# Neighbourhood attention on one core: key tiles of 9 row slots by 14 columns instead of 16 by 8

## The chip, the core and the metric

The kernel runs on one core of a Trainium2 chip. A core has a matrix engine (TensorE, PE in the profile, with its weight loads shown as PEld), a vector engine (VectorE, DVE), a scalar engine (ScalarE, ACT), GpSimd (POOL) and SyncE (SP). Each works through its own list of instructions in the order in which the kernel issues them, and they wait for each other through semaphores. [...] Transfers to and from HBM are issued by SP, POOL or ACT and are carried out by 16 DMA engines. The metric is the device time of one execution in microseconds, median over several runs.

## The reference

```
qkv = x @ wqkv                          # x: 224 x 224 x 192, bfloat16
r0 = clip(i - 6, 0, 224 - 1 - 12)       # first key row of query row i; columns alike
key rows    r0 + 0, 2, ..., 12          # 7 rows, dilation 2
key columns c0 + 0, 2, ..., 12          # 7 columns
logits = q . k * 192 ** -0.5            # 49 keys per query
p = softmax(logits)
out = (sum of p * v) @ wo
```

The keys of a query all have one row parity and one column parity. Rows 0 to 5 share the window that begins at row 0, and the last rows the one that begins at row 211.

## The kernel before

**Classes.** `rc` is the parity of the key rows, `cc` that of the key columns. Each class has 112 key rows (and columns) and 112 query rows: in the interior those of its own parity, at one border a few of the other parity too. Two neighbouring columns are folded into one position of 384 channels (three times 128), so that there are `S` = 112 positions in a row.

**Scores.** The weights are folded first: A = Wq·Wkᵀ·scale (the tiles `aw`), so that a logit is (x_q·A)·x_k and the keys are x itself. Keys lie with channels on partitions in `XA` (128 channels) and `XB` (64 channels and 64 rows of one-hot marks). Query products x_q·A lie in `GA` and `GB`; in `GB` the partitions beside the one-hot marks hold 0 or -30000, so the same two matmuls that make a logit also mask keys outside the window. A key tile has 16 row slots by 8 columns, 128 keys. A step treats 8 query rows of one class. Their windows need 14 key rows; two blocks of 8 rows form a ring of 16 slots. A key tile meets the queries of 8 + 6 = 14 positions: 14 x 8 = 112 columns of a matmul. `s_group` (L399, L400) computes four tiles into one PSUM bank, and ACT takes the exponential (L403). 14 tiles for each column class make seven such groups per step.

**Values.** `XN` holds x with keys on partitions. `y_unit` (L418) multiplies tile after tile with the exponentials and adds the overlapping position windows up in PSUM, for half of the positions, one column class and one part `kt` of the channels. There are eight such units per step; each is copied into `ysb` by ACT or DVE (L424). `o_mm` (L436) multiplies that by Wv·Wo (`WP`), whose further column gives the sum of the exponentials; DVE takes the reciprocal (L440) and multiplies (L451) into `o_sb`, which SP stores.

**Query products.** `g_piece` makes them in three pieces per step (kinds 0, 1, 2: L343, L351), and ACT and DVE copy them from PSUM (L355 to L365): kinds 0 and 2 to `GA` by ACT, the two halves of kind 1 to `GB` by DVE. Outermost positions pair with positions of the other column class, and are computed apart in `edge_item` (L287) and spread by `edge_copies`, with ACT (L321, L324) and POOL (L322, L323).

**Loads.** x comes in twice: transposed by SP into `xt` (L91), from which DVE and ACT copy the keys of a new block into `XA` and `XB` (`key_copy`, L269, L271), and straight into `XN` by POOL and SP (L103), 14 DMAs per block of 8 rows.

**PSUM.** Three pools have two buffers each: `ps_s` for scores, `ps_y` for y, and `ps_go`, whose buffers have two banks each, for query products, edge products and the projection's pieces in turn. A buffer is written again only when its copy has ended.

**Order.** The schedule is by hand: the instructions go to each engine in the order in which the Python loop emits them, and waits follow from that. The loop runs over 28 steps, the two row classes in turn. In each of the seven groups of a step stand one `s_group`, then a query piece or (L563 to L565) a piece of the step before's projection, and then one or two y units of tiles whose exponentials are done (`run_y`), so that PE meets S, a job, y, S, a job, y.

Of the kernel before, what the change touches and what calls it, by code (L numbers as in the profile page):

```python
# [7 lines left out]
BF = mybir.dt.bfloat16  # L8
# [8 lines left out]
BR = 8  # L17
KC = 8
QW = KC + HALO
NEG = -30000.0  # L20
XP = 448
SLOTS = 16
NO = 7
H0 = 63
# [3 lines left out]
def kernel(  # L28
# [11 lines left out]
    NJ = H // 16  # L40
    NK = S // KC
    SR = H // 2
# [23 lines left out]
    gkeys = [(rc, p, 0) for rc in range(2) for p in range(2)] + [(0, 0, 1), (1, (NJ - 1) % 2, 1)]  # L66
    GA, GB = {}, {}
    for gk in gkeys:
        for cc in range(2):
            if gk[2] == 0:  # L70
                GA[gk[:2] + (cc,)] = const.tile([128, S, BR], BF, name="ga%d%d%d" % (gk[:2] + (cc,)))
            GB[gk + (cc,)] = const.tile([128, S, BR], BF, name="gb%d%d%d%d" % (gk + (cc,)))

# [4 lines left out]
    def gkey(rc, j):  # L78
        border = (rc == 0 and j == 0) or (rc == 1 and j == NJ - 1)
        return (rc, j % 2, int(border))  # L80
# [4 lines left out]
    def load_xt(b, part):  # L85
        if not 0 <= b < NJ:
            return
        if b not in xt:
            xt[b] = xt_pool.tile([128, 3, 16, S], BF, name=f"xt{b}", tag="xt")
        r = 4 * part  # L90
        nc.sync.dma_start_transpose(out=xt[b][:, :, r:r + 4, :].rearrange("p t r c -> p t (r c)"),  # L91
                                    in_=xp[16 * b + r:16 * b + r + 4].rearrange("r j c -> (r j) c"))

    DOWN = list(range(NK - 1, -1, -1))

    def load_xn(eng, rc, m, tiles):

        if not 0 <= m < NJ:
# [11 lines left out]
    for part in range(4):  # L110
        load_xt(0, part)
    for part in range(4):
        load_xt(1, part)
    load_xn(nc.sync, 0, 1, DOWN[:7])
    for part in range(4):
        load_xt(2, part)
    load_xn(nc.sync, 1, 1, DOWN[:5])
# [5 lines left out]
    gorder = [(0, 0, 1), (1, 0, 0), (0, 1, 0), (1, 1, 0), (0, 0, 0), (1, (NJ - 1) % 2, 1)]  # L123
    assert sorted(gorder) == sorted(gkeys)
    i_r = const.tile([128, len(gorder), BR], I32, name="i_r")

# [5 lines left out]

# [4 lines left out]
    for gi, (rc, p, brd) in enumerate(gorder):  # L137
        j = (0 if rc == 0 else NJ - 1) if brd else 2 + p
        ws = [max(BR * j + i - HALO, 0) if rc == 0 else min(BR * j + i, SR - WIN) for i in range(BR)]
        for (a, n_, first, step) in _affine(ws):  # L140
            io(i_r[:, gi, a:a + n_], n_, first % 16, step, 16)


# [14 lines left out]
    t_r = const.tile([128, SLOTS], BF, name="t_r")  # L158
    rowT = const.tile([128, SLOTS, KC], BF, name="rowT")
    cm = const.tile([128, S], BF, name="cm")  # L160
    cmE = const.tile([128, S, BR], BF, name="cmE")
    rm = const.tile([128, len(gorder), BR], BF, name="rm")
    nc.vector.tensor_single_scalar(out=i_c[:], in_=i_c[:], scalar=31, op=ALU.bitwise_and)
    nc.vector.tensor_single_scalar(out=t_c[:], in_=i_c[:], scalar=0.0, op=ALU.is_equal)
    nc.vector.tensor_single_scalar(out=t_r[:], in_=i_c[:, 0:SLOTS], scalar=0.0, op=ALU.is_equal)
    nc.vector.tensor_copy(out=rowT[:], in_=t_r[:].unsqueeze(2).to_broadcast([128, SLOTS, KC]))
    nc.vector.tensor_single_scalar(out=i_m[:], in_=i_m[:], scalar=31, op=ALU.bitwise_and)
    nc.vector.tensor_scalar(out=cm[:], in0=i_m[:], scalar1=float(HALO) + 0.5, scalar2=NEG, op0=ALU.is_gt, op1=ALU.mult)
    nc.vector.tensor_copy(out=cmE[:], in_=cm[:].unsqueeze(2).to_broadcast([128, S, BR]))
    nc.vector.tensor_single_scalar(out=i_r[:], in_=i_r[:], scalar=15, op=ALU.bitwise_and)  # L170
    nc.vector.tensor_scalar(out=rm[:], in0=i_r[:], scalar1=float(HALO) + 0.5, scalar2=NEG, op0=ALU.is_gt, op1=ALU.mult)

    def onehots(eng, cc, rc):
# [5 lines left out]
        eng.tensor_copy(out=XB[cc][rc][c_].rearrange("p n (r c) -> p n r c", c=KC),  # L179
                        in_=t_c[c_].rearrange("p (n c) -> p n c", c=KC).unsqueeze(2).to_broadcast([32, NK, SLOTS, KC]))  # L180
        eng.tensor_copy(out=XB[cc][rc][r_],
                        in_=rowT[r_].rearrange("p r c -> p (r c)").unsqueeze(1).to_broadcast([32, NK, 128]))

    def masks(eng, gi, ccs=(0, 1)):
        for cc in ccs:
            g = GB[gorder[gi] + (cc,)]
            eng.tensor_copy(out=g[CROW[cc]], in_=cmE[CROW[cc]])
            eng.tensor_copy(out=g[RROW[cc]], in_=rm[RROW[cc], gi, :].unsqueeze(1).to_broadcast([32, S, BR]))

    def grp_copy(eng, rc):  # L190
        eng(out=XN[rc][:, 0:NK * XP].rearrange("p (n c) -> p n c", c=XP)[:, :, 0:64],
            in_=grp[:].unsqueeze(1).to_broadcast([128, NK, 64]))
        eng(out=XN[rc][:, NK * XP:], in_=grp[:])

    onehots(nc.vector, 0, 0)
    masks(nc.vector, 0, (0,))
# [464 lines left out]
```

## Time and profile before

| | us |
|---|---|
| median of 3 runs (331.49 to 335.01) | 334.75 |
| profiled execution: its span, first to last instruction | 332.4 |
| PE busy | 314.8 |
| DVE busy | 269.1 |
| ACT busy | 249.9 |
| POOL busy | 212.5 |

No time of the profiled execution other than its span is given. Busy time of PE runs from the first start to the modelled end of each matmul, which overlap; how fast PE really works is read from the starts of consecutive matmuls. "A <- B: total, times, longest" in the list of waits is idle time of A's engine that ended when B did. A group's line gives the engine, the operation, what it writes and reads with partitions x elements, the count, busy time in us, the mean of one in ns and the idle time before it. In the chain and in the timeline the first two numbers are start and length in us.

### The profile page before, as it was taken

The page shows a single profiled execution, that of the slowest core. Times are in us where ns is not written, and L with a number is a line of the kernel's source. Part 1 is how long each engine was busy: PE and PEld are TensorE (multiplying, and loading weights), DVE is VectorE, ACT ScalarE, POOL GpSimd, SP SyncE. Part 2 cuts the span into 40 slices and gives each one's busy share as a digit, 9 for nine tenths or more (in the row PEclk, how much of TensorE's full clock was granted, in tenths as well). Part 3 has the DMA queues.
Part 4 walks back from the last instruction along what each step waited for, and adds up shares of the span by engine and source line. Part 5 has one row for each costly group of instructions (what it writes and reads, how often), then busy time and mean ns, then how long its engine had stood idle before and what let it go on. Part 6 is the DMA issues. An engine that isn't in the chain of part 4 may idle for free.

```text
span 332.4 us, 12183 instructions
## 1 busy us (share of the span) xinstructions
PE 314.8 (95%) x4948; PEld 273.2 (82%) x4948; DVE 269.1 (81%) x538; ACT 249.9 (75%) x525; POOL 212.5 (64%) x438
## 2 busy tenths in 40 slices
PE   7999899599999999999999999999999999999980
PEld 4557887588988889888998889888898889988980
DVE  7757989489888998889888898889888898887771
ACT  5648678298887877897877878788887988888652
POOL 2887668546677667675676666686677666753072
PEclk9999999799999999999999999999999999999997
DMA  9999995988899998999889987999989944545233
GB/s 165 179 188 168 191 181 149 173 178 202 215 208 213 180 192 202 216 211 172 186 214 213 161 216 179 188 227 199 183 206 227 204 110 127 162 127 130 46 106 103
DMA packets 106391, 58.98 MB, mean 177 GB/s; under 512 B 93008, under 2 KB 100184, under 8 KB 106336
## 3 DMA queue, kind: packets, MB, share of 16 engines
q1 hardware_dynamic: 89010, 40.82, 64.2%
q0 software_dynamic: 16416, 16.74, 20.9%
q8 instruction: 38, 0.62, 0.8%
q10 hardware_dynamic: 910, 0.66, 0.8%
q14 instruction: 17, 0.14, 0.2%
HBM read 19.56 MB, written 19.27 MB: 117 GB/s over the span
## 4 chain that ended last, share of the span: by engine, by line
PE 73%; DMA 12%; POOL 5%; DVE 4%; issue 2%; SPq 1%; ACT 1%; POOLq 0%; DVEq 0%; ACTq 0%
PE y L418 19%; PE po L436 18%; PE pg L343 13%; DMA xn<-in_x_dram 10%; PE s_ps L399 9%; PE s_ps L400 9%; POOL xn L103 4%; PE pg L351 3%; DVE o_sb L451 2%; DMA xt<-in_x_dram 1%; PE pe L287 1%; SPq L91 1%; DVE ysb L424 1%; ACT ysb L424 1%; DVE rs L440 0%
## 5 line engine op out<-in xcount | busy, mean ns | idle before, releaser
L103 POOL DMA_DIRECT2D xn<-in_x_dram x332 | 185.9, 589 | 86.5 <-PE y L418 49.7
L403 ACT ACTIVATE p_sb<-s_ps 128x448 bf16<-128x448 f32 (+3 forms) x196 | 105.6, 539 | 21.6 <-PE s_ps L400 21.1
L418 PE MATMUL y<-p_sb,xn 128*128 128x112 bf16 (+5 forms) x1736 | 108.5, 207 | 4.8 <-DMA xn<-in_x_dram 3.9
L418 PEld LDWEIGHTS <-xn 128*128 128x128 bf16 (+1 forms) x1736 | 95.7, 97 | 18.1 <-issue 7.3
L424 ACT CAST ysb<-y 128x504 bf16<-128x504 f32 (+1 forms) x140 | 73.3, 544 | 38.7 <-PE y L418 35.4
L400 PE MATMUL s_ps<-gb,xb 128*128 128x112 bf16 (+4 forms) x812 | 99.9, 212 | 0.3 <-ACT gb L357 0.3
L399 PE MATMUL s_ps<-ga,xa 128*128 128x112 bf16 (+4 forms) x812 | 100.1, 212 | 0.0
L451 DVE TENSOR_TENSOR o_sb<-po,rs 128x768 bf16<-128x768 f32 x109 | 93.6, 858 | 5.6 <-DMA out_dram<-o_sb 0.4
L436 PE MATMUL po<-WP,ysb 128*128 128x193 bf16 x770 | 84.6, 249 | 1.2 <-DVE o_sb L451 0.5
L400 PEld LDWEIGHTS <-xb 128*128 128x128 bf16 (+1 forms) x812 | 77.2, 99 | 0.0
L399 PEld LDWEIGHTS <-xa 128*128 128x128 bf16 (+1 forms) x812 | 73.8, 99 | 1.9 <-issue 1.3
L343 PE MATMUL pg<-xt,aw 128*128 128x327 bf16 (+5 forms) x420 | 69.0, 297 | 1.3 <-DMA xt<-in_x_dram 0.4
L436 PEld LDWEIGHTS <-ysb 128*128 128x128 bf16 x784 | 64.3, 98 | 2.7 <-ACT ysb L424 1.1
L424 DVE CAST ysb<-y 128x392 bf16<-128x392 f32 (+1 forms) x84 | 49.7, 592 | 0.7 <-PE y L418 0.6
L343 PEld LDWEIGHTS <-aw 128*128 128x128 bf16 x420 | 31.2, 100 | 14.4 <-issue 1.2
L440 DVE RECIPROCAL rs<-po 128x4 f32<-128x4 f32 x110 | 19.4, 177 | 23.2 <-PE po L436 21.7
L357 DVE CAST gb<-pg 64x872 bf16<-64x872 f32 x27 | 28.6, 1058 | 7.2 <-PE pg L351 6.6
L355 ACT CAST ga<-pg 128x872 bf16<-128x872 f32 x28 | 24.8, 886 | 8.7 <-PE pg L343 8.7
L360 DVE CAST gb<-pg 64x848 bf16<-64x848 f32 x27 | 28.2, 1044 | 0.4
L365 ACT CAST ga<-pg 128x848 bf16<-128x848 f32 x28 | 24.2, 866 | 0.6 <-PE pg L343 0.3
L271 DVE COPY xb<-xt 64x896 bf16<-64x896 bf16 x56 | 22.9, 409 | 0.8
L269 ACT COPY xa<-xt 128x896 bf16<-128x896 bf16 x25 | 23.5, 940 | 0.0
(81 smaller groups left out, 152.0 us busy)
## 6 DMA issues: line engine op xcount, KB each, us to landing
xn<-in_x_dram POOLq DMA_DIRECT2D x332, 48.0 KB, 4.4
out_dram<-o_sb SPq DMA_DIRECT2D x25, 630.0 KB
xn<-in_x_dram SPq DMA_DIRECT2D x60, 48.0 KB
xt<-in_x_dram SPq DMA_TRANSPOSE x56
out_dram<-o_sb SPq DMA_DIRECT2D x50, 9.0 KB
out_dram<-o_sb SPq DMA_DIRECT2D x8, 78.8 KB
out_dram<-o_sb SPq DMA_DIRECT2D x25, 18.0 KB
out_dram<-o_sb SPq DMA_DIRECT2D x26, 6.0 KB
```

The lines of the kernel that those rows point to most:

```text
L103: eng.dma_start(out=XN[rc][p0:p0 + 64, XP * n + 64:XP * (n + 1)], in_=xp[r0:r0 + 15:2, KC * n:KC * (n + 1), :])
L343: nc.tensor.matmul(pg[:, a_:b_, 0:nq], lhsT=AW[w], rhs=xt[b][:, k, la:la + 2 * (b_ - a_ - 1) + 1:2, q0:q0 + nq], start=(a_ == ra if kind = ...
L355: nc.scalar.copy(out=A[0][:, 3:S, :], in_=pg[:, :, 0:nq].rearrange(v))
L357: mid(out=Bt[0][0:64, 3:S, :], in_=pg[0:64, :, 0:nq].rearrange(v))
L360: mid(out=Bt[1][64:128, HALO:S, :], in_=pg[64:128, :, 3:nq].rearrange(v))
L399: nc.tensor.matmul(o, lhsT=XA[rc][:, cc, n, 0:kn], rhs=a[:, lo:hi, :].rearrange(f), start=True, stop=False)
L400: nc.tensor.matmul(o, lhsT=XB[cc][rc][:, n, 0:kn], rhs=b_[:, lo:hi, :].rearrange(f), start=False, stop=True)
L403: nc.scalar.activation(out=p[0:kn, 0:off], in_=s_ps[0:kn, 0:off], func=ACTF.Exp)
L418: nc.tensor.matmul(y[:, BR * (a_ - h0):BR * (b_ - h0)], lhsT=XN[st.rc][kp, d:d + 128], rhs=p[kp, off + BR * (a_ - lo):off + BR * (b_ - lo) ...
L424: eng(out=o, in_=y[:, 0:BR * (h1 - h0)].rearrange("p (i n r) -> p i n r", n=NO, r=BR))
L436: nc.tensor.matmul(po[:, k, 0:C + 1], lhsT=st.ysb[cc][:, kt, n, :], rhs=WP[:, cc, kt, :], start=(kt == 0), stop=(kt == 1))
L451: nc.vector.tensor_tensor(out=o, in0=po[:, 0:k, 0:C], in1=rs[:, 0:k].to_broadcast([128, k, C]), op=ALU.mult)
```

## The change

A key tile has 9 row slots by 14 columns, 126 keys; the two other partitions are zeroed once. There are 8 tiles per column class. A **band** is three query rows of one class and needs the 9 key rows that the ring holds; a tile meets 14 + 6 = 20 positions, 20 x 3 = 60 columns (42 or 18 at the ends). There are 38 bands per class (the last has one row), 76 ticks of the main loop, the classes in turn. Each tick emits, for its band and the previous tick's band: S of column class 0 with one exponential of 462 columns (here **S0**), y of class 0 part 0 (**y00**), **S1**, **y01**, **y10**, the first job of the tick, **y11**, the loads of the class's next three rows into `XN`, the other jobs, and the key copies for the next band of this tick's class. y00, y10 and y11 are copied by ACT, y01 by DVE, all with 336 columns, into `YS`.

Query products, projection and output go by groups of three bands (nine rows). The second half of query kind 1 is copied by DVE, the first now by ACT. The edge copies are all on POOL. Jobs repeat every six ticks, from tick 4 on (`T0`):

| tick of six | first job | jobs after y11 |
|---|---|---|
| first | query kind 0, class 1 | edge product, edge copies, projection piece |
| second | query kind 1 | three projection pieces |
| third | query kind 2 | two pieces, store |
| fourth | edge copies (POOL) | query kind 0, class 0; piece, store |
| fifth | query kind 1 | none |
| sixth | query kind 2 | projection piece |

`XN` is loaded by POOL alone, one DMA of 14 partitions x 8 runs of 768 bytes per row (L103 before: 64 partitions x one run). `xt` blocks have 18 rows (16 before) and three buffers instead of four, and one transposing DMA brings six rows instead of four. The opening builds the masks and one-hot marks for the new shape; the special first step on 64 keys and the special last step with its own pieces and stores are gone.

```diff
-BR = 8
-KC = 8
+R = 3
+KC = 14
 QW = KC + HALO
+SL = 9
+KT = KC * SL
 NEG = -30000.0
 XP = 448
-SLOTS = 16
-NO = 7
-H0 = 63
+GR = 9
...
-    xt_pool = ctx.enter_context(tc.tile_pool(name="xt", bufs=4))
+    xt_pool = ctx.enter_context(tc.tile_pool(name="xt", bufs=3))
...
+    YS = {(rc, p, cc): const.tile([128, 2, 8, 128], BF, name=f"ys{rc}{p}{cc}")
+          for rc in range(2) for p in range(2) for cc in range(2)}
...
+    def load_xn(rc, t, eng):
+
+        if not 0 <= t < NT:
             return
-        p0 = 64 * (m % 2)
-        r0 = 16 * m + rc
-        for n in tiles:
-            eng.dma_start(out=XN[rc][p0:p0 + 64, XP * n + 64:XP * (n + 1)],
-                          in_=xp[r0:r0 + 15:2, KC * n:KC * (n + 1), :])
+        for i in range(trows(t)):
+            p0 = KC * (R * (t % 3) + i)
+            eng.dma_start(out=XN[rc][p0:p0 + KC, 0:NK * XP].rearrange("p (n c) -> p n c", c=XP)[:, :, 64:XP],
+                          in_=xp[2 * (R * t + i) + rc].rearrange("(n c) e -> c n e", c=KC))
...
+    def key_copy(rc, t, ea, eb):
+        if not 0 <= t < NT:
             return
-        t, k0 = xt[m], 64 * (m % 2)
-        v, d = "p r (n c) -> p r n c", DROW[cc]
-        ea(out=XA[rc][:, cc, :, k0:k0 + 64].rearrange("p n (r c) -> p r n c", c=KC),
-                       in_=t[:, 2 * cc, rc:16:2, :].rearrange(v, c=KC))
-        eb(out=XB[cc][rc][d, :, k0:k0 + 64].rearrange("p n (r c) -> p r n c", c=KC),
-                       in_=t[d, 1, rc:16:2, :].rearrange(v, c=KC))
-
-
-    GER = 24
+        m, l0, n = t // 3, 6 * (t % 3) + rc, trows(t)
+        k0 = KC * R * (t % 3)
+        rows = slice(l0, l0 + 2 * n - 1, 2)
+        ks = slice(k0, k0 + KC * n)
+        ea(out=XA[rc][:, :, :, ks].rearrange("p a n (r c) -> p a r n c", c=KC),
+           in_=xt[m][:, 0:3:2, rows, :].rearrange("p a r (n c) -> p a r n c", c=KC))
+        for cc in range(2):
+            d = DROW[cc]
+            eb(out=XB[cc][rc][d, :, ks].rearrange("p n (r c) -> p r n c", c=KC),
+               in_=xt[m][d, 1, rows, :].rearrange("p r (n c) -> p r n c", c=KC))
...
+            outs(mids[0], gb[0][0:64], pg[0:64], 0)
+            outs(mids[1], gb[1][64:128], pg[64:128], 3)
         else:
-            nc.scalar.copy(out=A[1][:, HALO:S, :], in_=pg[:, :, 0:nq].rearrange(v))
+            outs(nc.scalar.copy, ga[1], pg, 0)
...
+    def s_unit(st, cc):
+        rc, nr = st.rc, st.nr
+        a = GA[(rc, st.j % 2, cc)][:, st.k % 3]
...
+                nc.tensor.matmul(o, lhsT=XA[rc][:, cc, n, :], rhs=ra, start=True, stop=False)
+                nc.tensor.matmul(o, lhsT=XB[cc][rc][:, n, :], rhs=rb, start=False, stop=True)
                 st.p.setdefault((cc, n), []).append((lo, hi, p, off))
                 off += w
-        nc.scalar.activation(out=p[0:kn, 0:off], in_=s_ps[0:kn, 0:off], func=ACTF.Exp)
-
-    def y_unit(st, cc, h, kt, eng):
-        h0, h1 = HS[h]
-        kp = slice(0, 64 if st.first else 128)
+        nc.scalar.activation(out=p[:, 0:off], in_=s_ps[:, 0:off], func=ACTF.Exp)
...
+    def y_unit(st, cc, kt, eng):
+        nr = st.nr
...
+                nc.tensor.matmul(y[:, nr * lo:nr * hi], lhsT=XN[st.rc][:, d:d + 128],
+                                 rhs=p[:, off:off + nr * (hi - lo)],
...
+        r0 = R * (st.k % 3)
+        o = YS[(st.rc, st.j % 2, cc)][:, kt, 0:nn, 0:ni * gr].rearrange("p n (i r) -> p i n r", r=gr)[:, :, :, r0:r0 + nr]
+        eng(out=o, in_=y[:, 0:nr * S].rearrange("p (i n r) -> p i n r", n=nn, r=nr))
...
+    def o_mm(gp, ns):
+
+        po = ps_go.tile([128, 4, 256], F32, name="po", tag="go")
...
+    seq = [(0, 0), (0, 1), (0, 2), (1, 0)]
+    for q in range(NT - 3):
+        seq += [(0, q + 3), (1, q + 1)]
+    seq += [(1, NT - 2), (1, NT - 1)]
...
+    for i in range(0, NG - 1):
+        t = T0 + 6 * i
+        d = (0, 1, 2, 3, 3, 4, 5) if i else (2, 3, 4, 2, 4, 5, 5)
+        add_pg(t + d[0], 1, i + 1, 0)
+        if i + 2 < NG:
+            add_edge(t + d[0], i + 2)
+        add_ec(t + d[0], 1, i + 1)
+        add_pg(t + d[1], 1, i + 1, 1)
+        add_pg(t + d[2], 1, i + 1, 2)
+        if i + 2 < NG:
+            add_ec(t + d[3], 0, i + 2)
+            for kind in range(3):
+                add_pg(t + d[4 + kind], 0, i + 2, kind)
+    for rc, j in sorted(groups, key=lambda g: (g[1], g[0])):
+        e = seq.index((rc, min(3 * j + 2, NT - 1)))
+        d = (2, 3, 3, 4) if rc == 0 else (2, 4, 5, 6)
+        if grows(j) < GR:
+            d = (2, 2)
+        elif e + 6 >= N:
+            d = (2, 2, 3, 3)
+        for i in range(npieces[j]):
+            add_po(e + d[i], rc, j, i)
...
+    for ti in range(N + 4):
+        st = steps[ti] if ti < N else None
+        prev = steps[ti - 1] if 0 < ti <= N else None
+        jobs = go.pop(ti, [])
+        if st is not None:
+            s_unit(st, 0)
         if prev is not None:
-            if nxt is not None:
-                store(prev, [nc.sync])
-            else:
-                store(prev, [nc.sync, nc.gpsimd], parts=(0, 2, 3), cols=(4, NO))
-
-    last = steps[-1]
-    run_y((len(steps) - 1) * T + 7)
-    second = o_mm(last, (4, 5, 6), (0,))
-    run_y(10 ** 9)
-    o_out(*first)
-    o_out(*second, act=True)
-    store(last, [nc.gpsimd], parts=(1, 2))
-    for pool_, tag, nss in ((ps_s, "s", ((0, 1), (2, 3))), (ps_y, "y", ((4, 5), (6,)))):
-        pieces = [o_mm(last, ns, (1,), (pool_, tag)) for ns in nss]
-        for i, pc in enumerate(pieces):
-            o_out(*pc, act=i == 0)
-    store_piece(last, (0, 1), nc.scalar)
-    store_piece(last, (2, 3), nc.scalar)
-    store_piece(last, (4, 5, 6), nc.sync)
-    store(last, [nc.gpsimd, nc.sync], parts=(3, 0))
+            y_unit(prev, 0, 0, nc.scalar.copy)
+        if st is not None:
+            s_unit(st, 1)
+        if prev is not None:
+            y_unit(prev, 0, 1, nc.vector.tensor_copy)
+            y_unit(prev, 1, 0, nc.scalar.copy)
+        if jobs:
+            jobs[0]()
+        if prev is not None:
+            y_unit(prev, 1, 1, nc.scalar.copy)
+            if prev.rc == 1 or prev.k >= 2:
+                load_xn(prev.rc, prev.k + 1 + 2 * prev.rc, nc.gpsimd)
+        for f in jobs[1:]:
+            f()
+        if st is not None and (st.rc == 1 or st.k >= 2):
+            key_copy(st.rc, st.k + 1 + 2 * st.rc, nc.vector.tensor_copy, nc.vector.tensor_copy)
+        if ti >= T0 and (ti - T0) % 2 == 0:
+            load_xt((ti - T0) // 6 + 3, (ti - T0) % 6 // 2)
...
```

More of the change, by code (lines that the diff above doesn't have):

```diff
@@ new lines, in mm @@
+        def mm(part, w, k, piece, **kw):
+            (c, m, rows, b, l, n_, a) = piece
+            o = pg[part, c:c + m]
+            if rows:
+                nc.tensor.matmul(o.rearrange("p (r s) -> p r s", r=rows), lhsT=w, rhs=xt[b][:, k, l, a:a + n_], skip_group_check=True, **kw)
+            else:
+                nc.tensor.matmul(o, lhsT=w, rhs=xt[b][:, k, l, a:a + m], skip_group_check=True, **kw)
+        every = slice(0, 128)
+        for pcs in banks:
+            for i, (w, k) in enumerate(ws):
+                for n_, pc in enumerate(pcs):
+                    mm(every, AW[w], k, pc, start=(i == 0 and n_ == 0), stop=i == len(ws) - 1)
@@ L497 @@
         st = Step()
-        st.rc, st.j, st.p, st.first, st.o = rc, j, {}, not steps, None
+        st.rc, st.k, st.j, st.nr, st.p = rc, k, k // 3, trows(k), {}
         steps.append(st)
-    g_piece(0, 0, 0)
-    key_copy(0, 0, 0, nc.vector.tensor_copy, nc.vector.tensor_copy)
-    rest = g_piece(0, 0, 1, mid=nc.scalar.copy, later=True)
+    groups = {}
+    for rc in range(2):
+        for j in range(NG):
+            gp = groups[(rc, j)] = Group()
+            gp.rc, gp.j, gp.o = rc, j, None
```

553 lines of the change are left out of this document (286 added, 267 removed).

## The prediction

> **What bounds the kernel now.** I read the busy line first, then PE's own waits, then the chain that ended last, and last the timeline of one stretch of a step.
>
> ```profile
> span 332.4 us, 12183 instructions
> PE 314.8 (95%) x4948; PEld 273.2 (82%) x4948; DVE 269.1 (81%) x538; ACT 249.9 (75%) x525; POOL 212.5 (64%) x438
> ```
>
> ```profile
> PE y L418 <- DMA xn<-in_x_dram: 3.9, 1, 3.9
> PE fill L207 <- DVE ident L146: 1.6, 1, 1.6
> PE y L418 <- DVE ysb L424: 0.7, 1, 0.7
> PE po L436 <- DVE o_sb L451: 0.5, 1, 0.5
> ```
>
> All of PE's own waits, of which these are the first, add up to 9.4 us, and the largest is one late load of the opening. The chain of work that ended last is almost PE alone from 62.9 to 309 us, and the piece in it that comes once per step gives the step's time (start, length, what):
>
> ```profile
> 72.98 0.73 PE pg L343 x6
> ...
> 83.30 0.73 PE pg L343 x6
> 94.03 0.73 PE pg L343 x6
> ...
> 305.04 0.73 PE pg L343 x6
> ```
>
> From 72.98 to 305.04 lie 22 steps: 10.55 us per step of 8 rows. So 28 x 10.55 = 295.4 us are steps, PE-bound and without holes, and 37.0 us of the span are opening and end. ACT and DVE have slack, and two buffers per PSUM pool are enough, because between two y units (L418) there is always a piece of S and of other work, 1.4 us from y to y. The timeline, with the costs that I use:
>
> ```profile
> 155.35 0.21 PE L400 MATMUL s_ps<-gb,xb 128*128 128x112 bf16 x1
> 155.69 0.21 ACT L321 COPY ga<-ge 128x24 bf16<-128x24 bf16 x1
> 155.80 0.23 ACT L324 COPY ga<-ge 128x48 bf16<-128x48 bf16 x1
> 155.93 0.55 ACT L403 ACTIVATE p_sb<-s_ps 128x448 bf16<-128x448 f32 x1
> ```
>
> Where ACT is free, the exponential starts 0.31 us after the start of the last S matmul (150.06 to 150.37). Here that would be 155.66, yet it starts at 155.93, behind two copies that the program has before it: ACT works in program order.
>
> **PE's own work.** Starts of consecutive matmuls in the trace lie 49 ns apart at 112 columns, 28 to 29 at 64, 28 at 56 and 25 to 26 at 48. The change cuts key-by-query columns of S and y from 340,480 to 275,968, but raises their matmuls from 3360 to 5168. Per tick (one band of three rows) S and y have 68 matmuls: 52 of 60 columns (28 ns, between the 56 and 64 rows), 12 of 42 and 4 of 18. The last two have no row: on the line through 56 and 112 columns they cost 23 and 14 ns, at the 48 row 25 each; I take 25, the nearest row. That is 1.86 us per tick, 11.1 per six ticks, which make 18 rows. Now the step's 58 S and 62 y matmuls cost 5.38 us by the same spacings, 12.1 per 18 rows. [...] By the line alone the sum would be 0.07 us less per tick, 5 us in all.
>
> Projection: 64 matmuls of 86 ns per six ticks (5.5 us); 800 in all for 784. Query products (L343, L351): two groups, each now 5 column pieces instead of 3, with a tail of 33 to 88 columns: 0.87, 1.05 and 0.85 us for the three kinds, 5.5 us. Each kind 1 includes two changes of the weights' width, 0.09 and 0.08 us in the trace between L343 and L351. Edge product 0.45. **Sum 22.5 us per 18 rows, 1.25 per row, against 1.319 now: 15 us less over 224 rows** if PE never waits.
>
> **Where PE waits.** Now a tick is S0, y00, S1, y01, y10, first job, y11, other jobs. S0 0.44, y00 0.22, S1 0.47, y01 0.22 us. The two y buffers are used in turn, so y10 needs y00 copied out. That copy stands on ACT behind the exponential of S0. From rows: S0's last start 0.415 + 0.31 = 0.725; exponential of 462 columns, 0.46 to the next start (448 columns: 0.44); copy of 336 columns 0.44 (392: 0.489; 504: 0.581, so 0.82 ns per column over a fixed 0.17); ACT's end to PE's start 0.055 (trace). So y10 starts at 1.68 instead of 1.35: **0.33 us per tick, 25 us over 76 ticks**. Nothing covers it, as no job stands before y10. [...] Were the copy free to pass the exponential, those 25 us would be nothing.
>
> y11 likewise needs y01 copied by DVE, which is behind the key copies of the tick before (xa 672 elements and twice xb 336: some 0.65 us from L269's 0.39 and L271's 0.41 at 896; if the runs of 14 cost them that rate, 1.6, by the 1.04 ns per column of L424 on DVE). In the tick whose first job is edge copies on POOL alone nothing stands between y10 and y11: 0.65 us.
>
> **The jobs' buffers** are the larger part. Projection pieces, query products and the edge product share two buffers. A projection piece takes PE 0.69 us and DVE 1.08 (reciprocal 0.18 and L451 0.96, overlapped), so pieces in a row run at DVE's pace. In the second of the six ticks stand a query product of kind 1 and three projection pieces. Its two halves are copied by ACT (0.98) and then DVE (64x954, 1.15 by L357's 1.058 for 872), and the changed kernel's instruction order has DVE wait there for ACT; before, DVE did both. PE finishes the product at 2.9 us of that tick, ACT at 4.2, DVE at 5.4; the second piece waits for that buffer, the third for the first piece's division at 6.5. It ends at 7.25 instead of 4.85. The price of such holes is their length alone: after the one hole of 4.15 us at 57.4 the clock was lower (eight L436 matmuls took 1.29 us at 62.88, 0.68 later), but these are at most 1.3 us long. By the same count, PE work and time of the six ticks:
>
> first 3.9 → 4.7 (query product to 2.75, ACT's copy of it 2.95 to 3.95, edge product in the other buffer to 3.5; the projection piece needs the first buffer at 4.0), second 4.85 → 7.25, third 4.1 → 4.7, fourth 3.4 → 4.35 (y11), fifth 2.8 → 3.15, sixth 3.4 → 4.35 (the fifth ends at 3.15 but ACT is busy with it until 4.4, so the exponential comes 0.5 late, and y10 with it; DVE is 1.0 behind for y01). **Sum 28.5 us per 18 rows**, 6.0 of it waits.
>
> **Loads.** An xn DMA on POOL takes 0.55 to 0.6 us whether of 15 or 64 pieces (L461, L103), so three of 112 pieces take 1.8; 224 replace 332 on POOL and 60 on SP, which SP loses. The ring holds exactly three bands, so a band is fetched only when y11 of the same class has ended, and must be there at y00 two ticks later: 4.8 to 9.5 us by the table. Needed: 0.3 until POOL starts (y to L103), 1.15 to the third DMA, and 3.0 to 5.4 to land (4.4 median): 4.5 to 6.9. Only the fourth to sixth ticks are near; I take nothing, the bound is 2 us per six ticks. POOL's edge copies, now all its own, take some 3 us per six ticks and leave it under 60% busy. SP's order (transposes, then stores that wait for DVE) stays; three transposes replace four for more rows.
>
> **Sum.** 224/18 = 12.44 cycles x 28.5 = 354.5 us. Opening and end 37.0: the opening loads 14 rows of x less into xn (1.2 MB, 7 us at its 172 GB/s), while the last stores, one group in nine row-wise DMAs of 0.8 us each on SP, follow later (bounds -8 to +8, taken -2). Span 389.5. The runs' median (334.75) lies 2.35 above the span of 332.4 (no time of that execution beside it is given), so I carry some 1 to 2 us: **390 us**, 17% slower. The waits' bounds: zero (22.5) to those with slow key copies and late loads (30.5).
>
> **Rivals.**
> - *Likeliest, 0.66*: as above, 368 to 410.
> - *The tick's chain alone, 0.19*: the job buffers drain as they do now (only 0.5 us of such waits in the list above); what stays is y10's 0.33 per tick and y11's 0.65 per cycle, near 25.2 us per cycle: 313 + 35 + 2 = 350. Against it: DVE has 5.5 us of work in the second tick's 4.85.
> - *The ring of values binds, 0.06*: the load of xn ends PE's waits in the last three ticks of each cycle; 30.5 us per cycle gives 416. For it speaks the one 3.9 us wait for xn in the opening, against it that longer ticks give the loads time.
> - *Faster, 0.05*: PE stays the bound because the evictions keep up: 22.5 x 12.44 + 37 = 317 to 325. This is where ACT's copy would come before the exponential, or run in under 0.15 us; it turns at 23.8 us per cycle (1.319 x 18), so from 1.3 us of waits per cycle on the change is lost, and y10's alone are 2.0.
> - *Nothing to see, 0.04*: waits eat PE's gain and no more, 331 to 338. That the change does not do what it says is no case: the changed kernel's instruction order has the 5168 matmuls of 6 to 60 columns and the waits named here.
>
> A measurement of this kernel can tell about 1% from no change. Faster by over 1%: 0.05; within: 0.04; slower: 0.91. The range is 345 to 410, from the tick's chain alone to the top of the likeliest case.
>
> **What would show it.** PE busy in the changed profile must fall as a share, with PE's waits headed by y on ACT's copies and po or pg on DVE's divisions; the y10 group 0.3 us after y01 in every tick; a tick of 7 us in each six; ACT below 75%. Wrong if PE's waits stay under 20 us, if xn loads lead them, or if the six ticks are even.

## The result, and the profile after

The changed kernel takes 489.80 us (median of four, 482.88 to 493.08) where the kernel before takes 334.84: a ratio of 1.454, with a 95% interval of 1.441 to 1.467. Runs of one kernel fall into a faster and a slower group (here 482.88 and 488.04 us against 491.56 and 493.08); the medians here take in all of them, the ratios the faster ones alone, and the traces of e2, e2c and e11 are of the slower group. The direction was forecast, the size was not: 390 us was predicted, with 410 as the upper end.

The head of the page of the changed kernel (busy time and share of each engine; then, in 40 slices, PE's granted clock and the DMA engines' busy share in tenths):

```profile
span 486.3 us, 16299 instructions
...
PE 346.4 (71%) x7033; PEld 294.1 (60%) x7033; DVE 293.0 (60%) x634; ACT 299.9 (62%) x504; POOL 165.5 (34%) x414
...
PEclk9888989899789899799899699899799899999995
DMA  9994118639619817918918918918918917143232
```

No engine is the bound any more; PE was at 95%. The last row has a rhythm of three slices, 9, 1, 8: the DMA engines are busy for two slices and nearly idle for one, once per cycle of six ticks (36 us). The clock dips in the same rhythm. Something late happens once per cycle, and PE's waits name it:

```profile
PE y L497 <- ACT ys L504: 23.8, 58, 0.9
PE pe L344 <- DMA xt<-in_x_dram: 23.7, 9, 4.3
PE y L497 <- DMA xn<-in_x_dram: 20.6, 15, 4.0
PE y L497 <- DVE ys L504: 19.1, 15, 3.6
PE po L516 <- DVE gbp L439: 8.4, 7, 1.2
```

The first line is what the forecast spoke of (y10 behind ACT). The second and third are not: nine times, once per cycle, the edge product waits up to 4.3 us for the transposed x, and fifteen times y waits for xn. SP's own list through the end of that cycle (start, length of the issue, line, what) shows why the transposed x is late, and the chain of waits goes on from it:

```profile
255.59 3.66 SPq L536 DMA_DIRECT2D out_dram<-o_sb  x5
259.30 2.93 SPq L121 DMA_TRANSPOSE xt<-in_x_dram  x1
262.33 4.01 SPq L536 DMA_DIRECT2D out_dram<-o_sb  x5
266.39 7.83 SPq L121 DMA_TRANSPOSE xt<-in_x_dram  x2
```

```profile
254.61 0.96 DVE o_sb L526
...
266.39 8.99 DMA xt<-in_x_dram
275.37 0.04 issue
275.42 0.70 PE pe L344 x12
```

SP issued these one after the other, in the kernel's order. The first store waits for the last division of its group, which ends at 255.57, and issues five DMAs; behind it stands the second part of the transposed load, behind that the other class's store, and only at 266.39 the third part (with the next block's first part counted in one line). It lands at 275.4. PE needs it for the edge product, which stands in the first tick of the next cycle. After that hole PE is slow as well. The stretch from 276 to 279 us (columns: length, then busy time and count of PE, PEld, DVE, ACT and POOL, granted clock, DMA share, GB/s):

```profile
276.00:279.00 3.00, 3.00 (x48) 2.91 (x46) 1.97 (x6) 0.72 (x2) 0.81 (x4) 0.50 0.51 116
262.00:266.00 4.00, 3.20 (x84) 2.65 (x79) 2.66 (x5) 3.62 (x6) 1.68 (x3) 1.00 1.03 254
```

Clock 0.50 behind the hole, 1.00 ten microseconds before it.

The third surprise is in the groups by shape (columns: busy us, mean ns of one; then idle time before): the copy of 336 columns out of y, which the forecast put at 440 ns.

```profile
L504 ACT CAST ys<-y 128x336 bf16<-128x336 f32 x222 | 158.9, 716 | 42.5 <-PE y L497 36.2
L504 DVE CAST ys<-y 128x336 bf16<-128x336 f32 x74 | 53.0, 716 | 28.1 <-PE y L497 26.3
```

The forecast's 440 comes from the line through these two copies of the kernel before, which write their values in runs of eight:

```profile
L424 ACT CAST ysb<-y 128x504 bf16<-128x504 f32 x84 | 46.0, 581 | 27.8 <-PE y L418 27.8
L424 ACT CAST ysb<-y 128x392 bf16<-128x392 f32 x56 | 27.4, 489 | 10.8 <-PE y L418 7.5
```

### The profile page after: what moved, and what is told of

Read it like the earlier page. It is cut to its first block, busy times and chain, and to the rows that moved or that the text cites. A ratio compares the mean times of both kernels' runs of the same rounds, so it can differ in the third digit from the quotient of the medians.

```text
span 486.3 us, 16299 instructions
## 1 busy us (share of the span) xinstructions
PE 346.4 (71%) x7033; PEld 294.1 (60%) x7033; DVE 293.0 (60%) x634; ACT 299.9 (62%) x504; POOL 165.5 (34%) x414
## 2 busy tenths in 40 slices
DMA packets 95330, 59.18 MB, mean 122 GB/s; under 512 B 85554, under 2 KB 89106, under 8 KB 95258
## 4 chain that ended last, share of the span: by engine, by line
PE 26%; DVE 23%; DMA 19%; SPq 17%; ACT 9%; issue 3%; POOL 1%; ACTq 0%; DVEq 0%; POOLq 0%
DMA xt<-in_x_dram 15%; SPq L536 12%; PE po L516 8%; DVE o_sb L526 7%; PE y L497 6%; SPq L121 5%; PE pg L422 5%; ACT ys L504 4%; DMA xn<-in_x_dram 3%; ACT p_sb L485 2%; PE s_ps L482 2%; DVE gbp L439 2%; PE s_ps L481 2%; ACT gbp L439 2%; DVE ys L504 2%
## 5 line engine op out<-in xcount | busy, mean ns | idle before, releaser
L504 ACT CAST ys<-y 128x336 bf16<-128x336 f32 (+1 forms) x228 | 162.9, 715 | 44.0 <-PE y L497 37.6
L497 PE MATMUL y<-p_sb,xn 128*128 128x60 bf16 (+4 forms) x2584 | 122.5, 191 | 69.3 <-ACT ys L504 23.8
L497 PEld LDWEIGHTS <-xn 128*128 128x128 bf16 x2584 | 101.5, 100 | 86.0 <-issue 79.8
L485 ACT ACTIVATE p_sb<-s_ps 128x462 bf16<-128x462 f32 (+1 forms) x152 | 85.9, 565 | 91.5 <-PE s_ps L482 90.9
L516 PE MATMUL po<-WP,ys 128*128 128x193 bf16 x800 | 90.0, 258 | 17.2 <-DVE gbp L439 8.4
L481 PE MATMUL s_ps<-ga,xa 128*128 128x60 bf16 (+4 forms) x1292 | 96.2, 193 | 5.6 <-DVE xa L322 5.6
L526 DVE TENSOR_TENSOR o_sb<-po,rs 126x768 bf16<-126x768 f32 (+1 forms) x100 | 95.7, 957 | 4.8 <-DVE rs L522 0.2
L422 PE MATMUL pg<-xt,aw 128*128 128x327 bf16 (+8 forms) x525 | 87.9, 303 | 6.0 <-DVE aw L299 4.9
L481 PEld LDWEIGHTS <-xa 128*128 128x128 bf16 x1292 | 86.7, 101 | 5.9 <-issue 5.7
L482 PE MATMUL s_ps<-gbp,xb 128*128 128x60 bf16 (+3 forms) x1156 | 85.7, 193 | 0.0
L504 DVE CAST ys<-y 128x336 bf16<-128x336 f32 (+1 forms) x76 | 54.4, 715 | 28.1 <-PE y L497 26.3
```

The source lines that it names most:

```text
L422: nc.tensor.matmul(o.rearrange("p (r s) -> p r s", r=rows), lhsT=w, rhs=xt[b][:, k, l, a:a + n_], skip_group_check=True, **kw)
L481: nc.tensor.matmul(o, lhsT=XA[rc][:, cc, n, :], rhs=ra, start=True, stop=False)
L482: nc.tensor.matmul(o, lhsT=XB[cc][rc][:, n, :], rhs=rb, start=False, stop=True)
L485: nc.scalar.activation(out=p[:, 0:off], in_=s_ps[:, 0:off], func=ACTF.Exp)
L497: nc.tensor.matmul(y[:, nr * lo:nr * hi], lhsT=XN[st.rc][:, d:d + 128], rhs=p[:, off:off + nr * (hi - lo)], start=first, stop=True, skip_g ...
L504: eng(out=o, in_=y[:, 0:nr * S].rearrange("p (i n r) -> p i n r", n=nn, r=nr))
```

## The experiments

Theory: the late transposed load is a matter of SP's order; the slow copy is a matter of how it writes; the rest is the forecast's own sum. The rivals stand with each run. In the tables below, a tick is the time from its first S matmul to the next tick's, the median of nine cycles; the first tick is what is left of the median cycle. "Holes" are spacings of over 0.2 us between starts of consecutive matmuls, less 0.06 us each; the cycle's mean less its holes is called PE's own time.

**1. The transposed loads first** (e1). All three parts at the end of the first tick:

```
-        if ti >= T0 and (ti - T0) % 2 == 0:
-            load_xt((ti - T0) // 6 + 3, (ti - T0) % 6 // 2)
+        if ti >= T0 and (ti - T0) % 6 == 0:
+            for part in range(3):
+                load_xt((ti - T0) // 6 + 3, part)
```

> Edit: the three transposed loads of a block are all issued at the end of the first of the six ticks instead of at the end of the first, third and fifth, so that none of them stands behind a store on SP. Theory Q (SP's order): the third load comes late because SP works in order and stands at two stores, which wait for DVE and take some 4 us of issue each; without that PE's wait for xt (23.7 us over 9 times in the changed kernel) goes to nearly nothing, and with it the slow clock that follows each 3 us hole; a cycle of six ticks falls from 35.9 us to 31 to 32.5, the whole from 490 us to 440 to 455. Rival L (the loads themselves are slow): the landing of 9 us is the DMA engines' own, moved or not; PE's waits move to xn and xt and the time stays over 478 us. Rival C (the evictions on ACT and DVE bind anyway): the wait for xt vanishes but its time comes back as waits for ys and gb, 475 us or more.

Measured: 442.71 us, ratio to before 1.323 (1.311 to 1.335): 47 us less by the medians, 44 by the ratios. PE's list no longer has a wait for the transposed x, and that for xn is 14.0 us smaller:

```profile
PE y L497 <- ACT ys L504: 27.5, 67, 0.8
PE y L497 <- DVE ys L504: 17.3, 16, 2.3
PE po L516 <- DVE gbp L439: 8.0, 7, 1.2
PE y L497 <- DMA xn<-in_x_dram: 6.6, 6, 2.4
```

Theory Q holds, and the rivals L (slow landing whatever the order) and C (the waits come back on ACT and DVE, 475 us or more) fall. The mean cycle goes from 36.2 to 31.2 us: 3.5 us of that are holes, and 1.4 us is PE's own time, 23.5 before and 22.1 now. I put the 1.4 down to the slow clock behind the holes (mean granted clock 0.922 in the changed kernel, 0.969 here); that is an estimate, it was not measured apart.

**2. Longer written runs** (e2), **flat copies** (e2c), **and both edits** (e3). ys keeps band by band, so that a copy writes 14 x 3 values of one column tile in a row:

```
-        o = YS[...][:, kt, 0:nn, 0:ni * gr].rearrange("p n (i r) -> p i n r", r=gr)[:, :, :, r0:r0 + nr]
-        eng(out=o, in_=y[:, 0:nr * S].rearrange("p (i n r) -> p i n r", n=nn, r=nr))
+        o = YS[...][:, kt, 0:nn, ni * r0:ni * (r0 + nr)].rearrange("p n (i r) -> p n i r", r=nr)
+        eng(out=o, in_=y[:, 0:nr * S].rearrange("p (i n r) -> p n i r", n=nn, r=nr))
```

(The shorter last groups keep the old form.) Flat: `eng(out=YS[...] as one row [S * r0:S * (r0 + nr)], in_=y[:, 0:nr * S])`.

> Edit: the copies out of y write each column tile's 14 by 3 values in one run of 42 (84 bytes) where the changed kernel writes runs of 3 (6 bytes) nine apart; the rows of a group come out in another order, so the output's rows are permuted within a group of nine, and the work is the same otherwise. It reads y in runs of 3 (12 bytes). Theory W (short written runs are slow): a copy of 336 columns falls from 0.715 us to 0.42 to 0.50 on both ACT and DVE; PE's gap between y01 and y10 falls from 0.58 to about 0.33 us in every tick, and the whole by 76 x 0.25 = 19 us from that alone, up to 35 with y11's and the job buffers: 455 to 472 us. Rival P (short runs read from PSUM are as slow): the copy stays at 0.65 to 0.75 us and the time within 1% of 490. Rival X (the late transposes set each cycle's end): the copies get fast and the time stays above 480.

> Edit: the copies out of y read and write 336 elements in one run each; which value lands in which place of ys is then wrong, so the output is not the reference's, and the work is the same otherwise. Theory W: the same 0.42 to 0.50 us as with runs of 42, by the line through 392 and 504 columns of the kernel before 0.44. Rival P: only here, with no short run on either side, does the copy fall to 0.44. If it stays at 0.7 us even here, neither the written nor the read runs are the cause. Time as for the runs of 42, 455 to 472 us under theory W.

> Edit: both of the above, the transposes first and the written runs of 42 (rows permuted within a group). If the two causes are separate and add, 490 minus 40 minus 25 = 425 us (410 to 440) and a cycle of about 29 to 30 us, near the 28.5 of the forecast; the forecast's own terms (y10 behind the exponential 0.33 us per tick, the job buffers) would then be what is left. If one hides the other, 445 us or more.

Measured: 475.18, 471.35 and 433.55 us (ratios 1.420, 1.408 and 1.299). ACT's copies by shape, runs of 42, and then the flat copies:

```profile
L505 ACT CAST ys<-y 128x336 bf16<-128x336 f32 x216 | 94.7, 438 | 44.1 <-PE y L497 41.9 <-PE pg L422 0.5
...
L508 ACT CAST ys<-y 128x112 bf16<-128x112 f32 x6 | 4.0, 670 | 1.5 <-PE y L497 1.4
L508 ACT CAST ys<-y 128x336 bf16<-128x336 f32 x6 | 4.0, 663 | 0.7 <-PE y L497 0.6
```

```profile
L504 ACT CAST ys<-y 128x336 bf16<-128x336 f32 x222 | 97.2, 438 | 44.8 <-PE y L497 43.0
L504 ACT CAST ys<-y 128x112 bf16<-128x112 f32 x6 | 1.5, 252 | 2.2 <-PE y L497 2.2
```

Runs of 42 take 438 ns on ACT (508 on DVE), the flat copy the same 438 and 508; in e3 the runs of 42 take the same too. So for the price of the copy theory W holds and rival P falls: y is read in runs of 3 f32 in the first form and of 336 in the other. The lines of L508, the last groups' copies in the old form, show what the price hangs on: 112 runs of three take 663 (four apart; 716 where they lie nine apart), 112 runs of one 670, and the same 112 values in one run 252. In these lines it is the number of runs, not of elements: 112 runs take 663 to 716 with 336 elements and 670 with 112.

The time falls by less than expected: 14.6 us by the runs of 42 alone, where 18 to 35 was expected, and 9.2 on top of the first edit, not 25. The third to sixth ticks did get 0.22 to 0.36 us shorter, yet of nine cycles five took 30.5 to 34.2 us (two of these have the mask copies), the others 28.7 to 29.4. PE's list of that kernel says what came in the place of the copies' time:

```profile
PE y L497 <- DMA xn<-in_x_dram: 18.8, 16, 3.0
```

**3. The loads of xn left out** (e6, on e1; e9, on e3).

```
         if prev.rc == 1 or prev.k >= 2:
-            load_xn(prev.rc, prev.k + 1 + 2 * prev.rc, nc.gpsimd)
```

> Edit, on top of the transposes first: the loop's loads of xn are left out, so all later bands use the values of the first three (the weighted sums are of wrong rows; as much work for PE, ACT and DVE). Theory D (the forecast's bound for late xn loads was 25 us, taken at nothing): PE waits 9.6 us for xn in the steady part, in one or two holes of 2.6 us after which the clock is lower for some ticks; without the loads the time falls by 8 to 16 us, to 427 to 435, and every cycle is 30.4 us. If the time falls by more than 20 us the loads also slow something else (the transposes, the stores); if by less than 4, late xn is no cause of its own.

> Edit: the transposes first, the written runs of 42, and no loads of xn in the loop (later bands use the first three bands' values; rows permuted within a group; as much work for PE, ACT and DVE). It takes away the three terms that the forecast had sized too small or at nothing. Theory S (the forecast's other terms were sized right: PE's own 22.5 us, y10 0.33 us per tick, the job buffers, together 28.5 us per cycle): every cycle takes 28.5 to 29.2 us, 2 us under the mean of 31.0 with the loads, and the time falls from 433.6 to 410 to 416 us; the 20 us or so above the forecast of 390 are then the opening and the end. Rival: another wait takes the place of xn's and the cycle stays at 30 us or more, 425 us and above.

Measured: 435.15 us (ratio 1.310, 1.302 to 1.318) and 409.23 us (ratio 1.231, 1.223 to 1.239). On top of e1 either edit alone is worth little, 9.2 us for the copies and 7.6 for the loads (8 and 4 by the ratios, and the 4 is within the noise), but the two together 33.5 (31 by the ratios): a shorter tick mostly makes the load of xn late, as long as there are such loads. That is why the copies brought 9.2 of the 25 us expected in e3. In e9 the settled cycles are all 28.1 us, the two with mask copies 30.6 and 30.9. The tick table stands it against the forecast:

| tick | forecast | changed | e1 | e9 | e10 (below) |
|---|---|---|---|---|---|
| second | 7.25 | 8.00 | 7.70 | 7.20 | 6.69 |
| third | 4.70 | 4.94 | 4.94 | 4.63 | 4.32 |
| fourth | 4.35 | 4.95 | 4.97 | 4.36 | 4.36 |
| fifth | 3.15 | 3.53 | 3.53 | 3.24 | 2.99 |
| sixth | 4.35 | 4.55 | 4.56 | 4.03 | 4.08 |
| first | 4.70 | 10.5 | 4.89 | 4.66 | 4.14 |
| cycle | 28.5 | 36.4 | 30.6 | 28.1 | 26.6 |

Theory S holds, with cycle and time a little under its bands: with the three missing terms taken out, the rest of the forecast's sum is there tick by tick, within 0.1 us but for the sixth (0.3 less).

**4. Is xn late by the ring or by the transposed loads?** From the traces: a load of xn (three DMAs, one per row) starts 0.47 us after the start of the last y matmul that used the rows. From the first issue to the last landing it takes 4.0 us where nothing else moves, but 6.4 to 10.5 in the first tick of e3 while the transposed loads are under way (4.1 in the one cycle where none is in flight). Two runs: the transposed loads in three pieces over three ticks (e11, on the changed kernel), and left out from the fourth block on (e12, on e3).

```
-        if ti >= T0 and (ti - T0) % 2 == 0:
-            load_xt((ti - T0) // 6 + 3, (ti - T0) % 6 // 2)
+        if ti >= T0 and (ti - T0) % 6 < 2:
+            load_xt((ti - T0) // 6 + 3, (ti - T0) % 6)
...
         jobs = go.pop(ti, [])
+        if ti >= T0 and (ti - T0) % 6 == 2:
+            load_xt((ti - T0) // 6 + 3, 2)
```

```
+        if b >= 3:
+            xt[b] = xt[b - 3]
+            return
```

> Edit, on the changed kernel: the three transposed loads at the end of the first tick, the end of the second, and the start of the third, all ahead of the first store of the cycle on SP, but not in one burst as in the transposes-first kernel (442.7 us). Theory Q: what counts is to be ahead of the stores, so PE's wait for xt is gone here too: 435 to 447 us. Theory B (three transposes in a burst hold up the load of xn that the second tick waits for; there the holes before y00 of the second tick were 0.5 to 2.6 us, 7.7 us over nine cycles): those holes shrink to under 0.4 us each and the time is 3 to 8 us lower than 442.7. Rival: the second tick's holes stay as they are, so xn is late by the ring of nine rows alone.

> Edit: the kernel with the transposes first and the written runs of 42 (433.6 us), with the transposed loads of the fourth block on left out (later blocks use the first three blocks' tiles, so queries and keys are of wrong rows, and the rows are permuted within a group; as much work for PE, ACT and DVE); the loads of xn stay. There a load of xn took 6 to 10 us from its first issue to its last landing where transposes or stores were under way and 4 us elsewhere, and PE waited for it 0.5 to 3 us at y00 of the second, fifth and sixth tick. Theory M (the transposes in flight make the loads of xn slow): the loads issued in the first tick land in 4 to 5 us, the holes of the second tick go, the cycle falls from 31.0 to 28.1 to 29.5 us, the time to 410 to 420 us. Rival N (the ring of nine rows alone makes them late, as the load can't begin before y11 of the band that it replaces): the holes stay, 428 us or more. Between the two, 420 to 428: both, the transposes for the second tick and the ring for the fifth and sixth.

Measured: 446.16 us (439.04 to 448.97), not told apart from e1, and 421.43 us (ratio 1.268, 1.256 to 1.279), 12.1 us less than e3. In e11 the wait for the transposed x is gone as in e1, so being ahead of the stores is what counts; but the second tick's holes do not shrink (0.7 to 3.2 us in seven of nine cycles, 11.6 in all; 7.7 in e1), so it is not the burst. In e12 the loads issued in the first tick take 4.0 to 6.2 us, the second tick's holes before y00 are gone (11.9 us over nine cycles in e3), and PE's waits for xn fall from 18.8 us to:

```profile
PE y L500 <- DMA xn<-in_x_dram: 7.1, 11, 1.2
```

What stays are 1.1 us per cycle at y00 of the sixth and the first tick (the expectation miscounted these as the fifth and sixth), the ones that follow on short ticks. So it was both, as the middle case said, though 421.43 lies near its lower end: with transposed loads in flight the loads of xn took 6.4 to 10.5 us, without them 4.0 to 6.2, and the ring of nine rows has no slack where ticks are short (the 1.1 us per cycle).

**5. The first job before y10** (e4 on e1, e10 on e9).

```
             y_unit(prev, 0, 1, nc.vector.tensor_copy)
-            y_unit(prev, 1, 0, nc.scalar.copy)
         if jobs:
             jobs[0]()
         if prev is not None:
+            y_unit(prev, 1, 0, nc.scalar.copy)
```

> Edit, on top of the transposes first (442.7 us): a tick's first job stands between y01 and y10 instead of between y10 and y11. Theory F (the forecast's term: y10 needs the copy of y00, which on ACT stands behind the exponential of S0, and nothing covers it): the job covers it; in the trace of the transposes-first kernel y10 waits 0.59, 0.57 and 0.79 us in the third, fifth and sixth tick (in the fourth the first job has no work for PE, so nothing changes there, 0.58 and 1.0 stay), so 1.95 us per cycle, 23 us in all: 417 to 427 us. Rival G: ACT's copy of the query product now stands before the copy of y10, so y11, or y00 of the next tick, waits in its place: 433 us or more.

> Edit: the kernel of the run before, with the tick's first job between y01 and y10. There the wait of y10 that the forecast priced at 0.33 us per tick is to be seen without late loads. Theory F: in the third, fifth and sixth tick it is covered, so about 1 us per cycle and 12 us in all go: 399 to 405 us. Rival G (ACT's order gives it back: the copies of y10 and y11 now stand behind the query product's): within 4 us of the run before.

Measured: 434.32 us (ratio 1.308, 1.296 to 1.319), and 394.34 us (ratio 1.187, 1.178 to 1.195; 14.9 less than e9, a little more than the 12 expected). The first is 8.4 less than e1 by the medians, within the noise by the ratios; theory F had 16 to 26, and the time lies in rival G's band. In e9's timeline the wait is plain (columns: start, length; in brackets the idle time and its releaser):

```profile
248.79 0.56 ACT L485 ACTIVATE p_sb<-s_ps 128x462 bf16<-128x462 f32 x1
...
248.94 0.38 PE L497 MATMUL y<-p_sb,xn 128*128 128x60 bf16 x8
...
249.24 0.43 ACT L505 CAST ys<-y 128x336 bf16<-128x336 f32 x1
...
249.72 0.40 PE L497 MATMUL y<-p_sb,xn 128*128 128x42 bf16 x9 [0.40 <-ACT ys L505]
```

Exponential, then the copy of y00, then y10. This is a sixth tick, where ACT has the query product of the fifth before the exponential too, and the spacing from y01 to y10 is 0.58 us; in the other ticks it is 0.28. With the job in between, the third tick is 0.31 and the fifth 0.25 us shorter, and the second 0.51 and the first 0.52 too, where I had counted nothing.

The sixth is no shorter, and there rival G is seen. In e10 y10 no longer waits in it, but y00 does, in each settled cycle (spacing 0.53 us): the copy of the fifth tick's y10 now stands on ACT behind the query product's.

```profile
240.58 0.97 ACT L439 CAST gbp<-pg 64x981 bf16<-64x981 f32 x1 [0.54 <-PE pg L422]
241.45 0.77 ACT L505 CAST ys<-y 128x336 bf16<-128x336 f32 x2
...
241.94 0.38 PE L497 MATMUL y<-p_sb,xn 128*128 128x60 bf16 x8 [0.35 <-ACT ys L505]
```

In e4 the holes before y10 fall by 2.0 us per cycle, and those before y00 grow by as much, from 1.0 to 3.0: 0.6 of that stands in the sixth tick (rival G again), most of the rest are waits for xn, the same exchange as under 3. So where nothing waits for xn, theory F holds in the third and the fifth tick, and G in the sixth.

**6. The projection pieces spread** (e5), **and the edits that leave nothing out together** (e7: e4, e5, and the last two groups' stores taken in turns by SP's and ACT's queues).

```
-        d = (2, 3, 3, 4) if rc == 0 else (2, 4, 5, 6)
+        d = (2, 3, 3, 4) if rc == 0 else (2, 5, 6, 7)
```

> Edit, on top of the transposes first: the projection pieces of the second row class stand at offsets 2, 5, 6, 7 instead of 2, 4, 5, 6, so that the second tick has two of them instead of three and the fifth one instead of none. Theory J (the forecast's job buffers: in the second tick a query product waits for ACT and then DVE, and the pieces run at DVE's pace): the second tick falls from 7.5 to 5.7 to 6.3 us, the fifth grows from 3.5 to 4.2 to 4.6, so 0.3 to 1.1 us per cycle less: 430 to 439 us. Rival: the pieces' divisions are late on DVE wherever they stand, and the time stays within 1% of 442.7.

> Edit, on top of the transposes first: the job before y10, the pieces spread, and the last two groups' stores taken in turns by SP's and ACT's queues. If the gains add (some 20, 8, and 5 of the 15 us between the last matmul and the end): 403 to 415 us; under the rivals above, 430 or more. In no case below 340: PE's own work is 22.5 to 23.3 us per cycle, and the opening and the end take some 55 us here against 37 before.

Measured: 446.18 us (442.97 to 450.38), no gain over e1, as the rival had it, and 429.17 us (ratio 1.289, 1.276 to 1.301), between the cases. The second tick falls from 7.70 to 6.58 us, more than the 0.69 us of the piece that left it: the holes before the projection pieces in it go from 1.95 to 1.40 us in most cycles, so the buffers do hold it up. But the fifth grows by 0.68, the sixth by 0.41, and one cycle took 36.6 (PE stands still for 4.8 us of it, until just after a load of xn lands): the gain is given back. In e7 the time from the start of the last matmul to the end falls from 15.3 to 11.0 us by the second store queue; the rest of its gain is about e4's, not taken apart. It is the fastest of the kernels here that leave nothing out, 95 us above the kernel before.

## Why the prediction was wrong

Right in direction and in the terms that it wrote out; wrong because two transfers were taken at nothing, one copy was priced from the wrong kind of row, and opening and end were taken too short. From the forecast's span of 389.5 us to 486.3: 17.7 to e9's 407.2, 31.1 from there to e1's 438.3, and 48.0 to the changed kernel.

- **PE's own work, 22.5 us per 18 rows:** right. Cycle less holes is 22.1 in e1, 22.4 in e3 and e9. The spacings of 60, 42 and 18 columns, taken at 28, 25 and 25 ns, are 27 to 30, 25 to 28 and 25 in the changed kernel's trace at full clock.
- **"SP's order (transposes, then stores that wait for DVE) stays", costed at nothing:** the step that failed, and the largest, 48 us of span (44 by the ratios). The line says that the stores wait for DVE, and did not walk the queue: the third part stands behind two stores. From the first store to the third part's issue SP spends 10.8 us in the list above, the landing takes 9 more, and the edge product of the next cycle's first tick is the deadline: a block loaded in one cycle is wanted in the next. With the order changed, PE's waits for xt (23.7 us) go, and those for xn fall from 20.6 to 6.6. The change also took the fourth `xt` buffer away; no run tried four, but e1 and e11 show that with three the order alone is enough.
- **"The price of such holes is their length alone":** wrong for these holes, which are 2.0 to 4.5 us long where the forecast had 1.3 at most: behind 11 of 14 of them the granted clock was 0.50 to 0.70, while behind 16 of the 17 of 0.97 to 1.46 us it was 1.00. With the long holes PE's own time is 23.5 us per cycle, without them 22.1: over 12.67 cycles some 18 of those 48 us, by an estimate that puts all of it down to the slow clock.
- **The copy of 336 columns at 0.44 us:** mis-sized, 0.716 measured. The rows used (392, 504 columns) write runs of eight, these write runs of three. With runs of 42 the forecast's line is exact (0.438). DVE took 0.716 and 0.508 for the same two forms. Why a short run costs more, no run shows.
- **y10 behind the exponential, 0.33 us per tick:** right in kind. With the copy at 0.438 us the spacing from y01's last matmul to y10 is 0.28 us in most ticks of e9, with 0.716 it is 0.58; y11 in the fourth tick, forecast 0.65, is 0.70 and 0.99. A job in its place took 14.9 us off in e10, where nothing waits for xn.
- **The job buffers, second tick 7.25 us:** right (7.20 in e9, 8.00 in the changed kernel). That the tick falls by more than the piece that leaves it (e5) bears this out, and that its neighbours grow shows that moving the piece is no gain. In e9 the wait for DVE's half of the query product heads PE's list:

```profile
PE po L520 <- DVE gbp L439: 14.2, 9, 3.0
```

- **The loads of xn at nothing, bound 2 us per cycle:** mis-sized. From the first issue to the last landing the forecast had 4.2 to 6.6 us (1.15 to the third issue, 3.0 to 5.4 to land); it is 4.0 in a quiet stretch, but 6.4 to 10.5 in e3 where transposed loads are in flight. In the changed kernel PE waits 20.6 us for xn, in e1 6.6; once the ticks are as short as forecast, these loads cost 24.3 us (e3 to e9), the bound that I had given and not taken. So the "ring of values" rival was real, as a cost that a shorter tick calls up.
- **Opening and end, 37.0 - 2:** mis-sized, with what goes with them, by 22 us. By e9's trace the opening takes 31.0 us beyond its ten bands, the end 14.8 beyond its twelve (45.8 for 35.0); two cycles with mask copies on DVE are 2.6 us longer each (5.3); and 76 bands are 12.67 cycles, not 12.44, since the two last bands of one row take a tick each (6.3). Against it stands 4.7 us from a cycle of 28.1 instead of 28.5. This is read from the trace alone; of it only the end was tried (4.3 us, in e7).

Of what was to show it: PE's waits were headed by y on ACT's copies, the y10 wait came in most ticks, ACT fell below 75%, and the second tick was long. None of its three signs of being wrong came. But the first tick was longer still (10.5 us), which no case held.

Could the change win? PE's own 22.4 us x 12.67 and the 45.8 + 5.3 us of opening, end and masks make 335 us without any wait, by an estimate from e9's trace: the time of the kernel before. So even with the last of these waits gone the change would not win, unless the opening and the end shrink too.

## What to carry to other kernels

Walk the list of every engine that issues DMAs tick by tick, as one walks PE's: what stands ahead of a load, what that waits for, how long its issue takes (here two stores of 3.66 and 4.01 us), and when the load's first reader comes. Price a copy by the runs that it writes, from a row with runs as short (here 0.716 us in runs of three, 0.438 in runs of 42). And where a buffer has exactly as many slots as the window needs, the load into it can set a floor under the tick, as here: what is saved elsewhere comes back as a wait for that load (e3: 18.8 us against e1's 6.6; e4), so measure such causes together, not only one at a time.

## What was not expected of the hardware

- The copies from PSUM to bf16 took their time by the number of written runs where these were short: 112 runs of three or of one element 0.66 to 0.72 us on ACT, 8 runs of 42 0.438, one run of 336 0.438, and one run of 112 0.252. Reading f32 from PSUM in runs of three cost nothing on top (e2 against e2c, 0.438 both).
- The row loads of xn, 84 KB each, three per band, land 4.0 us after the first issue in a quiet stretch and 6.4 to 10.5 us after it beside transposed loads (e3), while the whole kernel moves only 137 GB/s on average (59.18 MB over 431.6 us).
- Behind holes of 2 to 4.5 us in PE's work the granted clock was mostly lower. In the changed kernel from 85 to 380 us there are 14 spacings of over 2 us between starts of matmuls; behind 11 of them the mean granted clock of the next 3 us was 0.50 to 0.70, behind the other three (2.3 to 2.5 us) 1.00. Behind 16 of the 17 spacings of 0.97 to 1.46 us in the same stretch it was 1.00; the other one, at 202.6, lies within 0.50 that began at 199.2.
